# Unused TensorE matmuls cut into 128-column pieces, and two output matmuls moved into a wait, at the start of a fused Sinkhorn attention and bilinear FFN kernel

## The chip, the cores and the metric

The kernel runs on one core of a Trainium2 chip. The metric is the device time of one execution in microseconds (us). The profile's span, from the first to the last instruction, is about 1.8 us shorter than that time (245.06 against 246.84 us before). Engines: PE is TensorE's matmul, PEld its weight load, DVE is VectorE, ACT is ScalarE, POOL is GpSimd.

## The reference, cut to what matters

```python
P = sort_net                               # (4, 8, 8, 8)
for _ in range(5):                         # "Sinkhorn": a serial chain on tiny data
    P = exp(P - max(P)); P /= sum(P, -1); P /= sum(P, -2)
k_sorted, v_sorted = P @ k_blocks, P @ v_blocks        # q, k, v: (4, 8, 768, 64)
attn = softmax(scale * q_block @ k_sorted_block.T)     # block by block, 96 rows
x = (attn @ v_sorted_block)                            # -> (3072, 512)
out = ((x @ w_a) * (x @ w_b)) @ w_out                  # d_ff 1536
```

Nothing can be mixed before the five Sinkhorn rounds are done. They take about 9 us on DVE and ACT (2.48 to 11.68 us in the trace of before) and use PE for nothing. After them PE works to the end.

## The kernel before

PE follows the program's order. While DVE and ACT do the Sinkhorn rounds, PE transposes the first q tiles (`turn_q`) and runs matmuls on a tile of zeros whose results nobody reads ("heat"), so that PE's clock is up when the work comes. In this kernel's trace heat matmuls of 512 columns start every 427 ns before the clock rises at 6.69 us ("cold") and every 216 ns after it ("warm").

```python
def keep_busy(ps, n, cols=512):
    for _ in range(n):
        nc.tensor.matmul(ps[:, 0:cols], lhsT=warm[:, 0:P], rhs=warm[:, 0:cols],
                         start=True, stop=True)
...
keep_busy(heat[:, 0], 8)
for it in range(5):
    nc.scalar.activation(out=p_nat, in_=p_nat, func=AF.Exp)
    if it == 2: turn_q(0, "act")           # PE transposes, ACT copies to SBUF
    if it == 3: turn_q(1, "act")
    if it == 4: turn_q(2, "act"); turn_q(3, "act")
    ...
    nc.vector.reduce_sum(out=rsum, ...); nc.vector.reciprocal(out=rsum, in_=rsum)
    if it > 0:
        nc.tensor.matmul(heat[0:NB, 1, 0:NB], lhsT=rsum, rhs=rsum, ...)  # ties heat to the chain
        keep_busy(heat[:, 0], (0, 4, 3, 2, 4)[it])
    ...                                    # normalise rows and columns
```

Then the first batch's attention runs, half of the blocks at a time, the four head pairs overlapped by hand:

```python
to_columns(0)                              # pc_ps: the Sinkhorn result reaches PE
half_mix(0, 0, "k", "act", fill=2, cols=256)
...                                        # mixh, sc, vs_ps, o_ps, xt_ps of pairs 0 to 3
half_scores(0, 3)                          # sc
half_v(0, 3)                               # vs_ps
half_x(0, 2, "act")                        # xt_ps, needs DVE's xph; ACT copies it to xT
half_o(0, 3)                               # o_ps
begun = [psF.tile(...) for _ in range(3)] + [psA.tile(...)[:, 0] for _ in range(2)]
for n, (m, w_sb) in enumerate(((0, w_a_sb), (0, w_b_sb), (1, w_a_sb), (1, w_b_sb), (2, w_a_sb))):
    if n == 3:
        half_x(0, 3, "act")
    ab_mms(begun[n], w_sb, 0, m, 0, range(KA - 1))   # pf: kc = 0, 1, 2 of 4
...                                        # FFN of batch 0 interleaved with the rest
```

`pf` needs the xT part of pair kc for its matmul number kc. So kc=2 waits for `half_x(0, 2)` and its copy on ACT.

The softmax here doesn't subtract the row's maximum and nothing guards it: scores larger than these inputs give would overflow.

## Time and profile before

| | before |
|---|---|
| time, median of 3 (lowest, highest) | 245.82 us (245.81, 246.04) |
| device time of the profiled execution (not one of the 3) | 246.84 us |
| its span | 245.06 us |
| PE busy | 236.8 us, 97% |
| Sinkhorn result reaches PE (first pc_ps matmul) | 12.33 us |
| PE pause inside the third sc group | 1.04 us |
| PE wait before the third xt_ps | 0.43 us |

The profiled execution took 1.0 us longer than the median: what is read from this trace is read from a slow sample, and the prediction was made from it.

The page's first line of busy time, and its chain of work that ended last by engine, say that PE is the limit. Each entry is busy us (share of the span) x instructions; the chain gives shares of the span.

```profile
PE 236.8 (97%) x2234; PEld 137.1 (56%) x2246; DVE 109.4 (45%) x258; ACT 104.5 (43%) x204; POOL 61.4 (25%) x88
...
PE 92%; DVE 4%; issue 1%; ACT 1%; DMA 1%
```

A saving therefore has to be found in a stretch where PE is idle, or where PE waits for the serial chain. Nearly all pauses of PE over 0.1 us stand in the first 25 us (after them come one of 0.18 us at 76.41 and the 3.3 us behind the last matmul, which the change does not touch). The chain in order of time (start, length, what held the end back) for 17 to 23 us:

```profile
17.75 0.25 PE o_ps L231 x8
18.00 0.23 PE sc L195 x6
18.23 1.04 issue
19.27 0.22 PE sc L195 x2
...
21.16 0.70 DVE xph L237
21.86 0.05 issue
21.90 0.34 PE xt_ps L222 x4
22.25 0.39 PE o_ps L231 x8
22.63 1.48 PE pf L332 x9
```

Look at 18.23. A group of eight sc matmuls stops after six, and no data passes between the sixth and the seventh. "issue" means that the profile shows nothing that PE waited for. The 21.16 line is the second loss: PE waits for DVE's xph. The PE timeline shows the same pause (start, length, line, what, count, [idle before <- releaser]):

```profile
17.93 0.30 PE L195 MATMUL sc<-qT,kT 64*128 64x96 bf16 x6
19.27 0.22 PE L195 MATMUL sc<-qT,kT 64*128 64x96 bf16 x2 [1.04 <-issue]
...
21.90 0.34 PE L222 MATMUL xt_ps<-ident,xph 96*128 96x96 bf16 x4 [0.43 <-DVE xph L237]
22.23 0.40 PE L231 MATMUL o_ps<-vs,eT 96*128 96x65 bf16 x8
22.47 0.66 PE L332 MATMUL pf<-xT,w_a_sb 128*128 128x384 bf16 x3
```

The page's DMA part also has a queue that carries instructions (queue and kind: packets, MB, share of 16 engines' span):

```profile
q8 instruction: 17, 0.28, 0.4%
```

17 packets of 16 KB (16384 bytes each in the DMA records), for 4480 recorded PE instructions: one per 264. The first starts 16.83 us after the span's start and ends at 17.80.

### The profile page before, as it was taken

Reading aid. Unit: us, or ns where it says so; the run is one execution under the profiler, and the core shown is the slowest. Engines: PE = TensorE matmul, PEld = TensorE weight load, DVE = VectorE, ACT = ScalarE, POOL = GpSimd, SP = SyncE. Lnnn points to the kernel's source line nnn. Section 1 sums busy time; section 2 is a strip of 40 time slices with the busy share of each in tenths; the row PEclk is TensorE's granted clock in tenths of the full one; section 3 lists DMA queues with packets and bytes.
Section 4 is the critical chain, followed back from the end, with each engine's and each line's share of the span. In section 5 each row is a group of like instructions: output and inputs, shape, how many; then the busy total and the mean of one; then the engine's idle time right before and its main releaser. Section 6 shows DMA issues by size and latency. Waiting matters only on the chain.

```text
span 245.1 us, 5487 instructions
## 1 busy us (share of the span) xinstructions
PE 236.8 (97%) x2234; PEld 137.1 (56%) x2246; DVE 109.4 (45%) x258; ACT 104.5 (43%) x204; POOL 61.4 (25%) x88
## 2 busy tenths in 40 slices
PE   7897999999999999999999999999999999999994
PEld 2375666566645466666654466666654465665442
DVE  6775366554536144364625144454525244444110
ACT  3664764467630055646440065646430133333001
POOL 8876478602240033250500053210000000000000
PEclk9999999999999999999999999999999999999999
DMA  5999999987998558986784358926223310000132
GB/s 80 201 199 197 198 199 201 202 114 78 160 149 197 133 106 132 162 128 89 106 141 121 118 96 125 169 45 67 43 79 118 118 45 0 0 3 1 43 128 86
DMA packets 53929, 28.02 MB, mean 114 GB/s; under 512 B 30736, under 2 KB 50960, under 8 KB 53904
## 3 DMA queue, kind: packets, MB, share of 16 engines
q0 software_dynamic: 20944, 14.16, 40.7%
q1 hardware_dynamic: 32816, 13.45, 27.4%
q8 instruction: 17, 0.28, 0.4%
q14 instruction: 8, 0.07, 0.1%
q10 hardware_dynamic: 144, 0.07, 0.1%
HBM read 28.32 MB, written 6.29 MB: 141 GB/s over the span
## 4 chain that ended last, share of the span: by engine, by line
PE 92%; DVE 4%; issue 1%; ACT 1%; DMA 1%
PE pf L332 51%; PE po L377 24%; PE mix L281 4%; PE o_ps L231 3%; PE sc L302 2%; PE mixh L180 2%; PE po L362 1%; PE vs_ps L208 1%; PE sc L195 1%; PE xt_ps L222 1%; DMA p_nat<-in_sort_net_dram 1%; PE heat L168 1%; PE two L332 1%; PE q_ps L260 1%; DVE xp L237 1%
## 5 line engine op out<-in xcount | busy, mean ns | idle before, releaser
L353 DVE TENSOR_TENSOR hT<-a_sb,pf 128x384 bf16<-128x384 bf16 x95 | 52.6, 553 | 73.8 <-PE pf L332 46.4
L332 PE MATMUL pf<-xT,w_a_sb 128*128 128x384 bf16 x380 | 77.9, 326 | 0.0
L332 PE MATMUL pf<-xT,w_b_sb 128*128 128x384 bf16 x380 | 77.5, 326 | 0.0
L352 ACT CAST a_sb<-pf 128x384 bf16<-128x384 f32 x95 | 45.5, 479 | 60.9 <-PE pf L332 41.3
L377 PE MATMUL po<-w_out_sb,hT 128*128 128x512 bf16 x265 | 61.3, 379 | 0.6
L332 PEld LDWEIGHTS <-w_b_sb 128*128 128x128 bf16 x384 | 37.5, 98 | 24.6
L332 PEld LDWEIGHTS <-w_a_sb 128*128 128x128 bf16 x384 | 34.9, 98 | 22.3
L377 PEld LDWEIGHTS <-hT 128*128 128x128 bf16 x276 | 26.3, 98 | 30.0
L162 ACT COPY o_sb<-po 128x512 f32<-128x512 f32 (+1 forms) x13 | 7.5, 578 | 46.8 <-PE po L377 45.2
L164 DVE COPY o_sb<-po 128x512 f32<-128x512 f32 (+1 forms) x12 | 7.9, 656 | 35.2 <-PE po L377 26.3
L307 ACT ACTIVATE eT<-sc 96x768 bf16<-96x768 f32 x24 | 18.1, 802 | 6.8 <-PE sc L302 6.8
L540 POOL COPY gate<-kT 1x1 bf16<-1x1 bf16 x8 | 1.4, 179 | 76.7 <-ACT kT L162 76.7
L237 DVE TENSOR_TENSOR xp<-o_ps,rec 96x512 bf16<-96x512 f32 x24 | 15.9, 684 | 0.6 <-DVE rec L235 0.2
L162 ACT CAST kT<-mix 128x384 bf16<-128x384 f32 x24 | 10.3, 482 | 7.9 <-PE mix L281 7.9
L95 POOL DMA_DIRECT2D k<-in_k_dram x16 | 11.6, 724 | 4.5 <-PE pf L332 2.3
L95 POOL DMA_DIRECT2D v<-in_v_dram x16 | 11.5, 722 | 3.5 <-DMA w_b_sb<-in_moe_w_b_dram 1.8
L231 PEld LDWEIGHTS <-eT 96*128 96x128 bf16 x256 | 10.3, 97 | 3.1 <-DVE xp L237 0.6
L235 DVE RECIPROCAL rec<-o_ps 96x8 f32<-96x8 f32 x32 | 5.6, 189 | 13.8 <-PE o_ps L231 13.8
L231 PE MATMUL o_ps<-vs,eT 96*128 96x65 bf16 x256 | 11.3, 193 | 0.2 <-DVE xp L237 0.2
L246 POOL COPY qc<-q 128x768 bf16<-128x768 bf16 x10 | 8.4, 843 | 7.5 <-DMA q<-in_q_dram 7.5
L168 PE MATMUL heat<-warm 128*128 128x512 bf16 x20 | 7.6, 525 | 1.4 <-DVE warm L77 1.3
L95 POOL DMA_DIRECT2D q<-in_q_dram x12 | 8.7, 721 | 1.3 <-DMA w_b_sb<-in_moe_w_b_dram 0.6
(80 smaller groups left out, 154.3 us busy)
## 6 DMA issues: line engine op xcount, KB each, us to landing
out_dram<-o_sb SPq DMA_DIRECT2D x17, 256.0 KB, 2.0
k<-in_k_dram POOLq DMA_DIRECT2D x16, 192.0 KB, 5.3
v<-in_v_dram POOLq DMA_DIRECT2D x16, 192.0 KB, 6.2
q<-in_q_dram POOLq DMA_DIRECT2D x12, 192.0 KB, 6.4
w_a_sb<-in_moe_w_a_dram POOLq DMA_DIRECT2D x6, 256.0 KB, 10.3
w_b_sb<-in_moe_w_b_dram POOLq DMA_DIRECT2D x6, 256.0 KB, 10.7
w_out_sb<-in_moe_w_out_dram POOLq DMA_DIRECT2D x3, 512.0 KB, 10.9
out_dram<-o_sb SPq DMA_DIRECT2D x12, 128.0 KB, 2.4
```

Of the source, the lines that this page charges most:

```text
L95: nc.gpsimd.dma_start(out=to, in_=_ap(t, base, [[W, P], [S * D, 2], [1, W]]))
L162: nc.scalar.copy(out=out, in_=in_)
L168: nc.tensor.matmul(ps[:, 0:cols], lhsT=warm[:, 0:P], rhs=warm[:, 0:cols], start=True, stop=True)
L231: nc.tensor.matmul(o_ps[:, e, i * (D + 1):(i + 1) * (D + 1)], lhsT=eT[:, hf, e, i * BLK:i * BLK + P], rhs=vs[0:BLK, i0 + i, V0 - 1 + e * ( ...
L237: nc.vector.tensor_tensor(out=_ap(xp, i0 * 2 * D, [[nxp * 2 * D, BLK], [D, 2], [2 * D, NBH], [1, D]]), in0=_ap(o_ps, 1, [[1024, BLK], [511 ...
L246: nc.gpsimd.tensor_copy(out=qc.rearrange("p c e d -> p e c d"), in_=loaded[g][2].rearrange("p e (c d) -> p e c d", c=NCH))
L281: nc.tensor.matmul(mix[e * D:(e + 1) * D, c // 3, c % 3 * P:(c % 3 + 1) * P], lhsT=src2[:, e, c * D:(c + 1) * D], rhs=s_all[:, 2 * g + e], ...
L307: nc.scalar.activation(out=eT[:, hf, :, 0:HB], in_=sc[0:BLK, :, 0:HB], func=AF.Exp, scale=float(scale))
L332: nc.tensor.matmul(pf[:, 0:HW], lhsT=w_sb[:, kc, m * P:(m + 1) * P], rhs=x_cols(b, kc, t), start=(kc == 0), stop=(kc == KA - 1))
L352: nc.scalar.copy(out=a_sb, in_=pf[:, 0:HW])
L353: nc.vector.tensor_mul(out=hT[:, m, t * HW:(t + 1) * HW], in0=a_sb, in1=ab[1][:, 0:HW])
L377: nc.tensor.matmul(held["po"], lhsT=hTs[b][:, m, c * P:(c + 1) * P], rhs=w_out_sb[:, m, :], start=(m == 0), stop=(m == KO - 1))
```

## The change

Two parts. The heat matmuls keep their total of columns but are cut into pieces of 128 columns: 84 matmuls instead of 21. And two of the `pf` matmuls (kc=0 and kc=1 of the first tile) are put ahead of `half_x(0, 2)`, to fill PE's wait for xph.

```diff
-            keep_busy(heat[:, 0], 8)
+            keep_busy(heat[:, 0], 32, P)
 ...
-                    keep_busy(heat[:, 0], (0, 4, 3, 2, 4)[it])
+                    keep_busy(heat[:, 0], (0, 16, 12, 8, 16)[it], P)
 ...
             half_v(0, 3)
+            begun = [psF.tile([P, 512], FP32, tag="F", name="pf")]
+            ab_mms(begun[0], w_a_sb, 0, 0, 0, range(2))
             half_x(0, 2, "act")
             half_o(0, 3)
-            begun = [psF.tile([P, 512], FP32, tag="F", name="pf") for _ in range(3)]
+            begun += [psF.tile([P, 512], FP32, tag="F", name="pf") for _ in range(2)]
 ...
-                ab_mms(begun[n], w_sb, 0, m, 0, range(KA - 1))
+                ab_mms(begun[n], w_sb, 0, m, 0, range(0 if n else 2, KA - 1))
```

Every matmul brings its own weight load, so part 1 adds 63 matmuls and 63 weight loads (2246 loads before): 126 PE instructions, all ahead of the first pc_ps matmul. Part 2 adds none.

## The prediction

> **What bounds the kernel.** TensorE: the page gives PE 236.8 of 245.1 us busy (97%), and 92% of the chain that ended last is PE. The change touches only the first 25 us. There the chain shows the Sinkhorn steps on DVE and ACT (2.5 to 12.3 us), a PE pause of 1.04 us marked "issue" inside one score group (18.23 to 19.27), and the timeline a PE wait for DVE's normalisation (21.40 to 21.90).

> **The pause.** Six of eight sc matmuls run, two wait; no data passes between them. [...] The DMA records show 17 instruction packets of 16 KB on one queue, one per about 256 PE instructions. By the program the pause comes after 447 PE instructions. If that is a boundary, the previous one lies at 191, executed at 13.1 us; the packet starts at 16.83, ends at 17.80, and PE goes on at 19.27. The next boundary (19.27) has its packet at 22.98. Both lag 3.7 us, so crossing to use takes about 6.2 us under this DMA load (200 GB/s), and 256 instructions take only 4.9 us here. I read the pause as a late instruction block, not hidden.

> **Part 1, small pieces.** 21 heat matmuls become 84: equal columns, 63 more matmuls and 63 more weight loads, all before 12.3 us. Block boundaries move 126 instructions earlier. The first is crossed in the fourth heat block, about 9.4 us; its successor is used up where o_ps of the first pair starts (15.5 us), and 9.4 + 6.2 = 15.6. The pause should shrink from 1.24 us between starts to 0 to 0.4, and PE is the chain there. The one after (crossed 15.6, ready 21.8, needed 22.6) just fits. Gain: about 1.0 us, a side effect of counting.

> The direct effect of the pieces is nil or a small loss. Cold, 512 columns start every 427 ns, so 128 take at least 107; warm, the nearest 128-column matmuls (vs_ps) take 83 ns against 54 for a quarter of 512. The warm blocks (12, 8, 16 pieces) fit into waits. The second block (16 pieces, cold until 6.7 us) stands before q_ps, whose copy on ACT already holds up the fourth exp by 0.34 us: what is lost there enters the chain. Estimate 0 to 0.6 us lost, 0.2 in the middle.

> **Part 2, two pf matmuls earlier.** They (2 x 163 ns) fit into the 0.50 us idle; their xT parts are ready at 21.02. But the third, kc=2, needs the ACT copy that ends at 22.76, and it started at 22.81 already. PE will idle after o_ps instead. Gain 0 to 0.05 us.

> **Sum.** 245.82 - 1.0 + 0.2 = 245.0 us; 8 in 10 between 244.3 and 246.1. Faster by over 2%: 0.02; within 2%: 0.97; slower: 0.01.

> **What would show it.** The "issue" pause near 18.2 us gone, at most a short one near 15.5; the first 16 KB packet of that queue 3 to 4 us earlier; q_ps of the first pair at 6.9 to 7.4 us; the wait before the third xt_ps mostly filled, and an equal new idle stretch before kc=2; from 27 us on the same trace, 0.8 us earlier.

> **What would make it wrong.** The pause is not instruction fetch, or moves without shrinking (then 246); cold pieces at 150 ns (then q_ps at 7.7 us, and the gain is gone); or PE's clock rises at another time than 6.7 us, which matmul spacing would show.

The exact 256 of its count was not measured when it was made: the trace it was read from gives one packet per 264 instructions, and only the shift by 256 below tests it.

## The result, and the profile after

| | before | after |
|---|---|---|
| first comparison, median of 6 | 245.93 (245.54 to 246.11) | 245.66 (244.99 to 246.17) |
| second comparison, another chip, median of 11 and 6 | 245.79 (245.77 to 246.59) | 245.05 (244.95 to 245.64) |
| span of the first profiled execution | 245.06 | 243.33 |
| first pc_ps matmul | 12.33 | 11.70 |
| pause inside the third sc group | 1.04 | none |

A ratio here is the mean time of one kernel's runs over that of the other's runs of the same rounds, so it is not quite the ratio of the quoted medians. The first comparison gave 0.9988, with a 95% interval of 0.9968 to 1.0007. The second gave 0.9964 (0.9950 to 0.9979). The gain is between 0.3 and 0.7 us by medians, and 0.55 to 0.82 us from fastest execution to fastest execution.

The page after (same parts as before): "issue" has fallen from 1% of the chain to 0%. PE reads 0.6 us busier in a span 1.7 us shorter, but that is no cost of the pieces: the trace before lacks 12 matmul records (2234 matmuls for 2246 weight loads), 11 of them of the late `po` matmuls (265 instead of 276).

```profile
PE 237.4 (98%) x2309; PEld 141.6 (58%) x2309; DVE 109.1 (45%) x258; ACT 104.4 (43%) x204; POOL 61.4 (25%) x88
...
q8 instruction: 18, 0.29, 0.5%
...
PE 93%; DVE 4%; ACT 1%; DMA 1%; issue 0%
```

The chain after, for the same work as shown of before:

```profile
17.13 0.25 PE o_ps L231 x8
17.38 0.28 PE sc L195 x8
17.66 0.33 PE vs_ps L208 x4
...
19.42 0.70 DVE xph L237
20.12 0.05 issue
20.17 0.36 PE xt_ps L222 x4
20.53 0.02 issue
20.55 0.49 ACT xT L162
21.04 0.04 issue
21.08 1.30 PE pf L332 x7
```

The eight sc matmuls now run in one piece. After xt_ps the chain leaves PE and goes through ACT's xT copy, which it did not do before: the kc=2 matmul now waits for that copy. The PE timeline of the kernel after:

```profile
17.31 0.34 PE L195 MATMUL sc<-qT,kT 64*128 64x96 bf16 x8
...
19.59 0.49 PE L332 MATMUL pf<-xT,w_a_sb 128*128 128x384 bf16 x2
20.17 0.34 PE L222 MATMUL xt_ps<-ident,xph 96*128 96x96 bf16 x4
20.50 0.40 PE L231 MATMUL o_ps<-vs,eT 96*128 96x65 bf16 x8
21.08 0.32 PE L332 MATMUL pf<-xT,w_a_sb 128*128 128x384 bf16 x1 [0.18 <-ACT xT L162]
```

So the two traces differ by 1.73 us, and two places hold nearly all of it: the pause (1.04) and an earlier arrival of the Sinkhorn result (0.63). But the timed medians differ by 0.27 and 0.74 us only: the execution traced before took 246.84 us, the one traced after 245.11, inside its own timed range. A single pair of traces does not answer for the mean; the experiments had to say which of the two places belongs to the change.

The second comparison was itself an experiment (the whole change again). Expected beforehand: fastest executions at 244.9 to 245.1 if part 2 does nothing, above 245.3 if part 2 costs. The fastest was 244.95.

### The profile page after: what moved, and what is told of

Same layout as the page of the kernel before. It is cut to its first block, busy times and chain, and to the rows that moved or that the text cites. A ratio compares the mean times of both kernels' runs of the same rounds, so it can differ in the third digit from the quotient of the medians.

```text
span 243.3 us, 5625 instructions
## 1 busy us (share of the span) xinstructions
PE 237.4 (98%) x2309; PEld 141.6 (58%) x2309; DVE 109.1 (45%) x258; ACT 104.4 (43%) x204; POOL 61.4 (25%) x88
## 3 DMA queue, kind: packets, MB, share of 16 engines
HBM read 28.32 MB, written 6.29 MB: 142 GB/s over the span
## 4 chain that ended last, share of the span: by engine, by line
PE 93%; DVE 4%; ACT 1%; DMA 1%; issue 0%
PE pf L332 52%; PE po L377 24%; PE mix L281 4%; PE o_ps L231 3%; PE sc L302 2%; PE mixh L180 2%; PE po L362 1%; PE vs_ps L208 1%; PE xt_ps L222 1%; PE sc L195 1%; DMA p_nat<-in_sort_net_dram 1%; PE heat L168 1%; PE two L332 1%; PE q_ps L260 1%; DVE xp L237 1%
## 5 line engine op out<-in xcount | busy, mean ns | idle before, releaser
L162 ACT CAST kT<-mix 128x384 bf16<-128x384 f32 x24 | 10.3, 482 | 8.0 <-PE mix L281 8.0
L168 PE MATMUL heat<-warm 128*128 128x128 bf16 x84 | 7.6, 264 | 1.3 <-DVE warm L77 1.3
```

The source lines that it names most:

```text
L162: nc.scalar.copy(out=out, in_=in_)
```

## The experiments

Each kernel was timed in up to six executions, and one of these was traced. All gave the correct output. Three theories were on the table. The fetch theory: the pause is a late block of PE instructions, and part 1 removes it by shifting the count. The clock theory: the time at which PE's clock rises differs from execution to execution and moves the span. The rival to both: the small pieces, or part 2, help directly.

### The kernel before once more

No edit.

> The kernel before, unchanged, for a second trace of it. Fetch theory: the pause inside a score group stands after the same 447 PE instructions, 0.9 to 1.3 us long, with the 16 KB instruction packet starting 3 to 4 us after instruction 191. Rival (the clock's rise is luck and sets the spread of single executions): in this trace the matmul spacing halves at another time than 6.7 us after the start, and the span differs from 245.1 by about as much as that time does, up to 1 us. If the rise comes at 6.7 us again and the span is 245.1 again, luck of the clock explains nothing.

Measured: median 246.56 us (246.06 to 246.60), against 245.82 (245.78 to 246.57) for eleven other executions of the same kernel on the same chip: ratio 1.0016, with an interval of 1.0004 to 1.0029. The interval excludes 1 though the kernels are identical, so intervals here are too narrow by at least that much. In the trace the clock rises at 6.46 us and the span is 244.80. The pause is in the same place, now 0.79 us long. There is one extra wait, for k's DMA, of about 0.1 us. And PE waits 0.75 us for the second q load, which landed at 10.15 us here and at 8.2 in the first trace; the heat matmuls behind it then run until the first pc_ps matmul at 12.09, although DVE's part of the Sinkhorn result was ready at 11.81. What follows: the pause is no accident of one execution, and the spread of 0.8 us between executions belongs to the kernel before as well.

### Part 1 alone

```diff
-            keep_busy(heat[:, 0], 8)
+            keep_busy(heat[:, 0], 32, P)
-                    keep_busy(heat[:, 0], (0, 4, 3, 2, 4)[it])
+                    keep_busy(heat[:, 0], (0, 16, 12, 8, 16)[it], P)
```

> Part 1 alone (84 small heat matmuls, no early pf matmuls). Fetch theory: no pause near 18 us, span as the kernel after within 0.1 us (243.3 to 243.5 when the clock rises near 6.0 us), time ratio to before as that of the whole change, 0.996 to 0.999. Rival (the early pf matmuls bring the gain): the ratio is 1.000 and the pause is still there.

Measured: median 245.09 us (244.98 to 245.68), ratio 0.9966 (0.9953 to 0.9979). No pause; clock rise at 6.08 us; span 243.33, that of the whole change to the last digit quoted. The ratio is at the low end of what was expected and better than the first one of the whole change. The PE timeline of part 1 alone around the third xt_ps:

```profile
20.17 0.34 PE L222 MATMUL xt_ps<-ident,xph 96*128 96x96 bf16 x4 [0.41 <-DVE xph L237]
20.50 0.41 PE L231 MATMUL o_ps<-vs,eT 96*128 96x65 bf16 x8
20.74 0.66 PE L332 MATMUL pf<-xT,w_a_sb 128*128 128x384 bf16 x3
21.24 0.49 PE L332 MATMUL pf<-xT,w_b_sb 128*128 128x384 bf16 x2
```

Compare with the timeline after: both kernels start xt_ps at 20.17, o_ps at 20.50 and the first w_b matmul at 21.24. The kc=2 matmul is here the third of three that start 0.163 us apart from 20.74, so at 21.07; after, it starts at 21.08. Part 2 only moved idle time from before xt_ps to before kc=2.

### Part 2 alone

```diff
+            begun = [psF.tile([P, 512], FP32, tag="F", name="pf")]
+            ab_mms(begun[0], w_a_sb, 0, 0, 0, range(2))
             half_x(0, 2, "act")
 ...                                       # as in the change; heat as before
```

> Part 2 alone (two pf matmuls early, heat matmuls of 512 columns). Fetch theory: the pause stays, 0.9 to 1.3 us, in the middle of the third score group; the wait before the third xt_ps is filled, and an idle stretch of 0.15 to 0.35 us opens before the pf matmul of kc=2; ratio 0.999 to 1.001. Rival (part 2 matters): ratio under 0.998.

Measured: median 245.81 us, ratio 1.0000 (0.9985 to 1.0015), fastest execution 245.78 as before's. The pause is there, 0.70 us, in the third sc group. This trace's clock rose at 4.87 us and its span was 244.02. Part 2 is worth nothing, as predicted, and it does not touch the pause. (The pause was shorter than the 0.9 expected: between two starts it measures 0.90, as idle time 0.70. In the kernel before these were 1.24 and 1.04.) The traced execution took 245.79 us, which is where most of before's executions lie, so 0.70 is the better figure for a typical execution than 1.04. Its chain:

```profile
17.29 0.23 PE sc L195 x6
17.52 0.70 issue
18.22 0.22 PE sc L195 x2
```

### 256 more instructions instead of 126

If the boundaries of instruction blocks are 256 apart, as the packets' spacing (257 and 264) suggests, a shift by 256 brings them back to where they were. Narrower pieces (64 columns on 64-column weights) give the count:

```diff
+    def keep_busy_small(ps, n):
+        for j in range(n):
+            p0 = j % 2 * PH
+            nc.tensor.matmul(ps[p0:p0 + PH, 0:PH], lhsT=warm[:, 0:PH], rhs=warm[:, 0:PH],
+                             start=True, stop=True)
 ...
-            keep_busy(heat[:, 0], 8)
+            keep_busy_small(heat[:, 0], 64)
 ...
-                    keep_busy(heat[:, 0], (0, 4, 3, 2, 4)[it])
+                    keep_busy(heat[:, 0], (0, 0, 0, 3, 16)[it], P)
+                    keep_busy_small(heat[:, 0], (0, 32, 24, 10, 0)[it])
```

> Heat matmuls still smaller (116 of them 64 columns wide on 64-column weights, the rest 128), so that PE has 256 instructions more than before ahead of the Sinkhorn matrix instead of 126: block boundaries fall again at the same places of the later program. Fetch theory: the pause is back inside the third score group, 0.7 to 1.3 us, after 447 + 256 PE instructions; span about 1 us longer than that of pieces alone at the same clock rise. Rival (small pieces themselves remove the pause, by whatever means): no pause, span as pieces alone.

Measured: the pause is back, 0.92 us, after the same six of eight matmuls. Counting PE's records in the trace, the one after the pause is number 704; in part 2 alone it is 448 (447 before it, as the prediction counted). The difference is 256. The chain of this kernel:

```profile
18.42 0.23 PE sc L201 x6
18.66 0.92 issue
19.58 0.22 PE sc L201 x2
```

Median 246.26 us, ratio 1.0019 (1.0000 to 1.0037), span 245.37. The span is not a clean comparison: the first heat block, now of narrow pieces, ended at 2.9 us (4.87 in before), PE idled for 1.9 us, and the clock rose only at 12.87 us. The verdict rests on the pause alone. More and smaller pieces with the pause back: it is the count that matters, not the size. (The expectation's 116 was a slip: 130 of the 149 heat matmuls are 64 columns wide.)

### 24 and 48 more instructions, in the first heat block only

```diff
-            keep_busy(heat[:, 0], 8)
+            keep_busy(heat[:, 0], 4)               # 24 more
+            keep_busy(heat[:, 0], 16, P)
```

```diff
-            keep_busy(heat[:, 0], 8)
+            keep_busy(heat[:, 0], 32, P)           # 48 more
```

> Heat as before, but the first block as 4 matmuls of 512 and 16 of 128: 24 PE instructions more ahead. Fetch theory: boundary instruction 191 falls at old instruction 167, executed near 11.9 to 12.6 us, the block is usable 5.8 to 6.2 us later and the next boundary falls at old instruction 423, inside o_ps of the second pair: a pause of 0.3 to 0.9 us stands there, shorter than before's 0.9 to 1.24, and no longer in the score group. Rival (the pause belongs to the score group, a hidden wait): it stays in the score group.

> Heat as before, but the first block in 32 pieces of 128: 48 PE instructions more ahead, all of it in the first block, which ends before the Sinkhorn chain needs PE. Fetch theory: the first boundary falls at old instruction 143, near 9.9 to 10.6 us, the block is usable by 16 to 16.8 and needed at about 16.6: pause 0 to 0.2 us, and nearly the whole gain of pieces alone (fastest executions 245.0 to 245.2). Rival (the small pieces of the later blocks bring the gain): fastest executions at 245.7 as before.

Measured, 24 more: no pause at all, neither in the score group nor in o_ps; span 243.25, fastest execution 244.93, median 245.01. One execution took 247.85, at a mean granted clock of 0.993; it is why the ratio is 0.998 (0.9947 to 1.0014). The chain where the pause was:

```profile
17.32 0.28 PE sc L195 x8
```

This trace is the cleanest pair with that of part 2 alone: the clock rose at 4.66 and 4.87 us, the first pc_ps came at 11.65 and 11.62, they differ in the first heat block and in part 2's order, which comes behind the place of the pause, and only the shifted kernel has no pause. The expected pause of 0.3 to 0.9 us was a miss. The block came earlier than I had reckoned: its packet starts at 13.94 us, 1.65 us after PE reaches instruction 191, not 3.7.

Measured, 48 more: no pause, fastest execution 244.91, median 245.27, ratio 0.9971 (0.9957 to 0.9984). In the traced execution the clock rose at 6.88 us, the Sinkhorn result came at 12.26, and the span was 243.89. The small pieces of the later heat blocks are not needed: the first block is enough.

### 12 more instructions

The miss suggested that a block is asked for some instructions before the point at which I had put it. A very small shift tells the two readings apart.

```diff
-            keep_busy(heat[:, 0], 8)
+            keep_busy(heat[:, 0], 6)
+            keep_busy(heat[:, 0], 8, P)
```

> Heat as before, but the first block as 6 matmuls of 512 and 8 of 128: only 12 PE instructions more ahead. In the traces so far the first packet does not lag instruction 191 by a constant 3.7 us; it starts 3.3 to 4.3 us after PE executes about instruction 160[...]. If so, the ask falls at old instruction 148, in the last heat block (10.3 to 11.0 us), the packet starts near 14.3 to 14.8, the block is usable by 16.7 to 17.2, and the next boundary, at old instruction 435 (the first sc matmul of the third group), is reached at 17.2: pause 0 to 0.3 us, fastest executions 244.9 to 245.1. Rival (my earlier reading, asked at instruction 191): 179 is executed near 12.5 to 12.9, usable near 19: pause about 1.0 us at the start of the third score group, fastest executions at 245.7.

Measured: a pause of 0.17 us at the boundary, before the first sc matmul. The profile's timeline puts it down to o_ps, which the sc matmuls do not read; the chain has it as issue:

```profile
17.02 0.26 PE o_ps L231 x8
17.28 0.17 issue
17.45 0.35 PE sc L195 x8
```

Span 243.38, fastest execution 245.14 (0.1 to 0.2 us above the kernels without a pause), median 245.42, slowest 246.26, ratio 0.9987 (0.9969 to 1.0005). In this trace, twelve instructions, eight small matmuls in place of two, take away most of the pause. The reading "asked at instruction 191" is refuted (it wanted about 1 us). The DMA records of the traces, with the time at which PE started the matmul of instruction 170 (its 85th matmul) and the one whose weight load is instruction 191 (its 96th):

| kernel (instructions added) | packet starts | instruction 170 | lag | instruction 191 | lag |
|---|---|---|---|---|---|
| before (0) | 16.83 | 12.99 | 3.8 | 13.15 | 3.7 |
| 12 more | 15.20 | 11.63 | 3.6 | 12.32 | 2.9 |
| 24 more | 13.94 | 10.30 | 3.6 | 12.29 | 1.7 |
| 48 more | 13.40 | 10.02 | 3.4 | 10.76 | 2.6 |
| after (126) | 11.27 | 8.12 | 3.2 | 8.96 | 2.3 |
| 256 more | 8.80 | 5.48 | 3.3 | 5.75 | 3.1 |

On that estimate it is no surprise that so little is enough. Before, instruction 170 stands in the first dense group behind the Sinkhorn chain. With 12 more ahead the same count is reached at the first pc_ps matmuls, with 24 more in the last heat block, in front of PE's wait for the chain. Instruction 170 then comes 1.4 and 2.7 us earlier in these traces (about 0.7 of it because the whole chain ran earlier there: first pc_ps at 11.60 and 11.65 against 12.33).

### The clock's rise, moved on purpose

```diff
-            keep_busy(heat[:, 0], 32, P)
+            keep_busy(heat[:, 0], 4, P)            # on top of the whole change
```

> The whole change, but the first heat block cut from 32 pieces to 4, so that PE idles until 5.0 us (70 PE instructions more ahead than before instead of 126, which still removes the pause). Clock theory: the clock rises after 8.3 us instead of 4.7 to 6.9, q_ps runs cold, its copy on ACT delays the exponentials, pc_ps comes 0.8 to 1.8 us later than 11.7, the span is longer by the same: 244.2 to 245.1 us, time 245.9 to 246.9, and no pause. Rival (the rise does not set the spread): span 243.3 to 243.6 as the whole change.

The 8.3 us can be had from earlier traces, as an estimate: dense heat was to begin at 5.0 us instead of 1.27, and the earliest rise traced by then, 4.66, moved by as much stands at 8.4.

Measured: clock rise at 8.41 us, first pc_ps at 12.35 (0.65 later than after's 11.70), no pause, span 243.96, times 245.72 to 245.98 (median 245.82, ratio 0.9996, 0.9983 to 1.0008). The direction is as expected. The size is below the range: I had put 0.8 to 1.8 us on pc_ps and 244.2 at least on the span. In the timeline q_ps starts at 6.84 instead of 6.51, and its twelve matmuls, run cold, take 0.85 us instead of 0.53. The fourth exponential, behind ACT's copy of q_ps, starts at 8.43 instead of 7.77, and that 0.66 reaches pc_ps. A clock that rises at 8.41 costs about two thirds of a microsecond against one that rises at 6.02.

### Filling the new idle stretch, and less heat before q_ps

The trace after shows how part 2 could have paid: kc=2 waits for ACT, while the second tile's kc=0 and kc=1 wait for nothing.

```diff
+            ab_mms(begun[1], w_b_sb, 0, 0, 0, range(2))
             for n, (m, w_sb) in enumerate(...):
 ...
-                ab_mms(begun[n], w_sb, 0, m, 0, range(0 if n else 2, KA - 1))
+                ab_mms(begun[n], w_sb, 0, m, 0, range(0 if n > 1 else 2, KA - 1))
```

> The whole change, and the first two matmuls of the second pf tile (kc=0, 1, weights w_b) put before the kc=2 matmul of the first tile, to fill the idle stretch that part 2 opened (after: o_ps starts at 20.50, kc=2 at 21.08, 0.18 us idle before it). Theory: the idle stretch is what part 2 lost again; filled, all later PE work comes 0.15 to 0.25 us earlier than in the whole change at the same clock rise, fastest executions 244.75 to 244.9. Rival (something behind, the xph of the last pair or the PSUM tiles, holds the chain): no change against the whole change.

> The reordered version again, beside the one with the shorter heat block and for a second trace. Fastest executions 244.7 to 244.85, median 244.8 to 245.0, ratio to before 0.994 to 0.997; the pf matmuls after o_ps without idle, the fourth xt_ps at 21.9 to 22.0 when the clock rises by 6.2 us.

Measured: medians 244.84 and 244.89 us, ratios 0.9953 (0.9940 to 0.9967) and 0.9959 (0.9945 to 0.9972), spans 243.07 and 242.94. The timeline of the first:

```profile
20.53 0.41 PE L231 MATMUL o_ps<-vs,eT 96*128 96x65 bf16 x8
20.77 0.49 PE L332 MATMUL pf<-xT,w_b_sb 128*128 128x384 bf16 x2
21.11 0.32 PE L332 MATMUL pf<-xT,w_a_sb 128*128 128x384 bf16 x1
```

The kc=2 matmul (at 21.11) no longer has idle time ahead of it, and the two w_b matmuls are already done. That is worth 0.2 to 0.3 us, and it stays to the end of the span. The fourth xt_ps of the second trace starts at 21.83 us, a little ahead of the 21.9 expected (22.21 in the kernel after).

The last version also cuts the second heat block, which stands in front of the first q_ps:

```diff
-                    keep_busy(heat[:, 0], (0, 16, 12, 8, 16)[it], P)
+                    keep_busy(heat[:, 0], (0, 10, 12, 8, 16)[it], P)
```

> The reordered version with the second heat block cut from 16 pieces to 10, so that even cold (107 ns each) it ends at 6.1 us, before the first q lands (6.2), and a late rise of the clock no longer holds up q_ps by the heat matmuls. Clock theory: q_ps starts at 6.2 to 6.3 whatever the rise; the fastest executions are as the reordered version's (244.74 to 244.84) or up to 0.1 lower, the slow ones (over 245.1) fewer. Rival: q_ps waits for its data and then runs cold, and less heat makes the rise later: no gain, or slower than the reordered version.

Measured: median 244.66 us (244.63 to 244.85), ratio 0.9950 (0.9937 to 0.9962), span 242.96. On the same chip the reordered version had 244.89 (244.72 to 245.22). It has the best median of all kernels tried and the narrowest spread, 0.22 us, over five executions. Two builds of one kernel differed by 0.74 us in median above, so 0.23 us does not show that the cut helps. In its trace q_ps starts at 6.29 us and waits for its data, no longer for heat; but that trace's clock rose early (5.31), so whether the cut helps in executions with a late rise was not traced.

## Why the prediction was right or wrong

For all traces the span can be taken apart. "Clock rises" is the start of full clock in the trace's clock record; the spacing of the matmuls halves there (107 to 56 ns at 6.02 in the kernel after). The mean clock that the profile gives does not show the rise: it reads 1.00 for 0 to 4.95 us of the kernel after, in which 128-column matmuls started every 107 ns. All times in us; "rest" is span minus pc_ps minus pause.

| kernel | clock rises | first pc_ps | pause | span | rest |
|---|---|---|---|---|---|
| before | 6.69 | 12.33 | 1.04 | 245.06 | 231.69 |
| before, again | 6.46 | 12.09 | 0.79 | 244.80 | 231.92 |
| part 2 alone | 4.87 | 11.62 | 0.70 | 244.02 | 231.70 |
| 256 more | 12.87 | 12.74 | 0.92 | 245.37 | 231.71 |
| after | 6.02 | 11.70 | 0 | 243.33 | 231.63 |
| part 1 alone | 6.08 | 11.71 | 0 | 243.33 | 231.62 |
| after, again | 5.77 | 11.69 | 0 | 243.32 | 231.63 |
| 12 more | 4.55 | 11.60 | 0.17 | 243.38 | 231.61 |
| 24 more | 4.66 | 11.65 | 0 | 243.25 | 231.60 |
| 48 more | 6.88 | 12.26 | 0 | 243.89 | 231.63 |
| after, late clock | 8.41 | 12.35 | 0 | 243.96 | 231.61 |
| reordered | 6.20 | 11.73 | 0 | 243.07 | 231.34 |
| reordered, again | 5.71 | 11.61 | 0 | 242.94 | 231.33 |
| reordered, shorter heat | 5.31 | 11.63 | 0 | 242.96 | 231.33 |

With the order of part 2 or without it, the rest is 231.6 to 231.7, but for the second trace of before with its late loads of k and q. The reordered kernels have 231.3. Everything else is the start of the first pc_ps matmul and the pause.

- **The pause as a late instruction block: right.** It is gone in every traced kernel shifted by 24 to 126 instructions (70 in the late-clock kernel), and back at 256. The traces show 16 KB a packet, and the stops of two kernels 256 instructions apart (number 704 with 256 more, 448 in part 2 alone). At that boundary PE stood for 0.70 to 1.04 us, with DMA at 197 to 200 GB/s in that stretch (12 to 24 us of before). That PE waited for the packet is inferred from counts and times; no record names it. In the kernel after, the packet ended at 12.24 us (5.6 us earlier than before, where 3 to 4 had been predicted), and PE reached instruction 448 at 14.89 without a stop: 2.65 us of room, where PE had gone on 1.3 to 1.5 us after the packet's end in two traces that paused (19.27 against 17.80 in before, 18.22 against 16.96 in part 2 alone).
- **Its size: right for the trace it was read from.** About 1.0 us was predicted; 0.70 to 1.04 were measured, and 0.70 in the one paused trace whose time (245.79) is typical.
- **When the block is asked for: wrong step.** The prediction put the request at instruction 191 (counting the program's PE instructions) and made "crossing to use" 6.2 us. The lags of 2.9 and 1.7 us with 12 and 24 more refute a fixed 3.7 from there; by my estimate the request comes earlier, near instruction 170. The prediction's result held because 126 is far more than needed.
- **Direct cost of the pieces: mis-sized, 0.2 us predicted, none measured.** I took the warm figure from vs_ps, 83 ns: in the chain, 0.33 us for a group of four. Within these groups the matmuls start 55 to 67 ns apart (trace of before). Heat pieces start every 107 ns cold and every 56 ns warm, a weight load each included, so a piece costs about a quarter of the 427 and 216 ns of a 512-column one. PE's busy time up to 4.95 us is 3.60 us with 8 large matmuls and 3.59 with 32 small ones. So q_ps started at 6.51 in the kernel after, not at 6.9 to 7.4.
- **Part 2: right, mechanism and size.** Its ratio alone is 1.0000. The idle stretch went where the prediction said, before kc=2.
- **Not foreseen: the clock.** I treated the rise at 6.7 us as fixed and named it only as a risk. It came at 4.9 to 6.7 us in the three traces of kernels with before's heat. From the earliest rise to the latest, q_ps moved from 6.26 to 6.86 and pc_ps from 11.62 to 12.33. Of these 0.71 us only about 0.4 can be the clock's: the fourth exponential, held up by ACT's copy of q_ps, moved by 0.44 (7.68 to 8.12), and 0.08 of that stood at the third already (5.92 to 6.00). The other 0.28 is DVE's copy `p_rep`, which took 0.56 us in before's first trace and 0.28 in eleven others. It also took longer, 0.39 and 0.37, with 48 more instructions and with the shorter heat; in all three traces it ended 0.08 to 0.09 us after a DMA-issuing instruction of POOL that overlapped it. Whether that held it up was not tested. So the 1.73 us between the first two traces were 1.04 of pause and 0.63 of earlier Sinkhorn result, of which the clock can account for about 0.3 and `p_rep` for 0.28. The late-clock kernel shows by intervention that the clock's path costs time (0.65 us with a rise at 8.41).
- **The sum.** 245.0 us was predicted, a gain of 0.8. The first comparison gave 245.66 (gain 0.27 by medians), the second 245.05 (gain 0.74), part 1 alone 245.09 (gain 0.73). That the sum came so close to the last two is partly luck: it took 1.0 us for the pause, read from an execution of 246.84 us, and 0.2 us for the pieces, which cost nothing measured. The typical pause of 0.70 less nothing gives nearly the same as 1.0 less 0.2.

What stays open: the first comparison's slow executions of the kernel after (246.00 and 246.17, spans 244.2 and 244.4) have no trace. They are longer than the late-clock kernel's trace (243.96), so a late rise alone may not cover them. A longer `p_rep` would add up to 0.3 us. A pause that sometimes comes back would, but none was seen in five traces with these heat pieces (after twice, part 1 alone, reordered twice). The same holds for the slowest execution with 12 more instructions. Nor did any run lower the DMA traffic, so that the traffic makes the block late is argued, not shown.

## What to carry to other kernels

When PE stops inside a group whose matmuls do not depend on each other, and the profile says "issue", count instructions to the stop and look for instruction packets in the DMA records; a few cheap instructions added ahead of an earlier wait can take the stop away (here 24, of a stop of 0.70 to 1.04 us). Moving work into a wait gained nothing here (ratio 1.0000), as the next step behind it hung on the same producer: move the work that waits for nothing into the new gap as well (here worth 0.2 to 0.3 us). And where the clock's rise differs between executions (here 4.87 to 6.69 us in three traces with before's heat), compare parts of the span that it cannot touch, or several traces, before believing a difference of under one microsecond.
